# Three small tiles laid behind eight operand tiles, and a norm factor kept in PSUM, in an attention and feed-forward kernel on Trainium2

## The chip, the cores and the metric

The kernel runs on one core of a Trainium2 chip, in one launch. The metric is the device time of the launch in microseconds (us), lower is better. The engines have short names: PE (TensorE) multiplies, PEld is its loading of weights, DVE (VectorE) and ACT (ScalarE) work on tiles, POOL (GpSimd) too, and SP (SyncE) issues the DMAs.

## The reference

Three parts follow each other. First is attention in which a query sees only the keys of its own cluster; its output is laid out as 1536 tokens by 512. The two feed-forward parts are, cut to what matters:

```python
def _moe_ref(x, w_in, w_out):                    # w_in 512 x 2048, w_out 2048 x 512
    h = x @ w_in
    g = np.where(h >= 1, h, np.where(h <= -1, 0.0, (h + 1) ** 2 / 4))
    return g @ w_out

def _moe2_ref(x, w_gate, w_val, w_out, rms_g):   # w_gate, w_val 512 x 1536, w_out 1536 x 512
    rms = np.sqrt(np.mean(x * x, axis=-1, keepdims=True) + 1e-06)
    xn = x / rms * rms_g
    g = xn @ w_gate
    silu = g * (1.0 / (1.0 + np.exp(-g)))
    return (silu * (xn @ w_val)) @ w_out
```

## The kernel before

All inputs are float32. A matmul of the feed-forward parts is made of three in a reduced float format: each operand is split into a high and a low part, and high x high, high x low and low x high are added in PSUM. So `proj` (L577) makes one 128 x 512 block of `h` from 12 matmuls: four slices of the 512 features, three products each. The 1536 tokens stand in three blocks of 512; XH and XL hold the high and low part of the activations.

A split weight slice, or a split block of activations between the two matmuls of a part, lies in an operand place: 128 partitions x 2 x 512 words, which is 4096 bytes of a partition. There are 26. Eighteen are cut out of the tiles `aa` and `bb` that attention used; the other eight, `place0` to `place7`, are tiles of their own in the pool `pf`. That pool is opened when attention ends, on the memory that attention's tiles had (`reuse_waits="tile"`: who first writes a new tile waits for the last users of the old tiles under it). Before the places the pool holds the running output `Y` (24576 bytes of a partition), and three small tiles: `gain` (16 bytes, the four columns of rms_g), `eps6` and `ones` (4 bytes each). Each takes a slot of 32 bytes. Behind the places come the tiles `a`, `raw`, `mid`, `bits` and `s`.

A weight slice arrives by two DMAs from SP's queue (`raw` and `mid`, L509 and L511) and is split by five DVE instructions and one of ACT (L524 to L540). A scheduler written by hand interleaves these with the units of matmuls; the order of every engine is fixed when the program is built, and the engines are held together by semaphores.

Between the two feed-forward parts stands the norm. For each block of 512 tokens, ACT squares the four slices of Y (L700), POOL adds them into one tile `s` (L706), ACT and POOL split the sum (L708, L709), and `norm_unit` lets PE add over the partitions with a matmul by ones into a PSUM bank `ssq` (L716). From it ACT makes a first value of the factor 1/rms in `s` (L722, L723, between two loads of its function table, L746), and DVE refines it by one Newton step (L728 to L730). `scale_unit` multiplies the four slices of Y by the gain and the factor (DVE, L737), and ACT and POOL split them into XH and XL (L738, L739). Block 0's scaling stands among the last units of the first part, blocks 1 and 2 among the first units of the second. A unit of the second part computes a gate and a value block (two PSUM banks of the four with tag `h`) and closes with ACT's sigmoid (L595), two multiplications of DVE (L599 with the gate's bank, L600 with the value's), and the split (L602 on ACT, L606 on DVE). The bank `ssq` is one of the four with tag `y`.

Of the kernel before, what the change touches and what calls it, by code (L numbers as in the profile page):

```python
# [10 lines left out]
F32R = mybir.dt.float32r  # L11
BF16 = mybir.dt.bfloat16
AF = mybir.ActivationFunctionType
ALU = mybir.AluOpType
# [15 lines left out]
NPLACES = 26  # L30
# [7 lines left out]
def clustered_attention_two_ffn(  # L38
# [14 lines left out]
    nc = tc.nc  # L53
# [65 lines left out]
    st = {}  # L119
# [342 lines left out]
    a, b, c = prep(0), prep(1), prep(2)  # L462
# [26 lines left out]
    free = []  # L489
# [204 lines left out]
    def block(x, j, b):  # L694
        return x[:, j, BLK * b:BLK * b + BLK]
# [15 lines left out]
    def norm_unit(b):  # L711

        total = fp["tp"](f"ssq{b}")
        pace["rate"] = 0.9
        for n, x in enumerate((XH, XL)):
            nc.tensor.matmul(total, fp["ones"].to_broadcast([128, 128]), block(x, 0, b), start=(n == 0), stop=(n == 1))  # L716
        r = st["r", b] = st["sq", 4 * b]

        def first():
            if b == NB - 1:  # L720
                tables("natural_log_exp_and_others")
            nc.scalar.activation(r, total, AF.Ln, bias=fp["eps6"], scale=1.0 / DM)  # L722
            nc.scalar.activation(r, r, AF.Exp, scale=-0.5)  # L723
            if b > 0:
                tables("sigmoid_and_others")

        def newton():
            nc.vector.scalar_tensor_tensor(total, total, DM * 1e-6, r, op0=ALU.add, op1=ALU.mult)  # L728
            nc.vector.scalar_tensor_tensor(total, total, 0.5 / DM, r, op0=ALU.mult, op1=ALU.mult)
            nc.vector.scalar_tensor_tensor(r, total, 1.5, r, op0=ALU.subtract, op1=ALU.mult)  # L730

        later.insert(0, (first, newton))

# [11 lines left out]
    def tables(name):  # L745
        nc.scalar.preload_act_table_set(name)  # L746

    def units():
# [14 lines left out]
        def norm(b):  # L763
            return (lambda: norm_unit(b), 0.45, 2.04, [], 0)
# [327 lines left out]
    pf = ctx.enter_context(tc.tile_pool(name="ffn", bufs=1, reuse_waits="tile"))  # L1092
    psf = ctx.enter_context(tc.tile_pool(name="psf", bufs=1, space=PSUM, reuse_waits="tile"))
    fp["Y"] = pf.tile([128, 4 * NB, 512], F32, name="Y")
    fp["gain"] = pf.tile([128, 4], F32, name="gain")
    nc.sync.dma_start(fp["gain"], rms_g)
    nc.scalar.mul(fp["gain"], fp["gain"], -1.0)
# [1 line left out]
    nc.gpsimd.memset(fp["eps6"], 1e-6)  # L1099
    fp["ones"] = pf.tile([128, 1], F32R, name="ones")  # L1100
    nc.scalar.copy(fp["ones"], ones[:, 0:1])
    for j in range(NPLACES - 18):
        t = pf.tile([128, 2, 512], F32R, name=f"place{j}")
        free.append(t)
    fp["raw"] = lambda n: (pf.tile([128, 512, 2], U32, tag="raw", bufs=2, name=f"raw{n}"),
                           pf.tile([128, 512, 2], U32, tag="mid", bufs=2, name=f"mid{n}"),
                           pf.tile([128, 512], U32, tag="bits", bufs=2, name=f"bits{n}"))
# [53 lines left out]
```

## Time and profile before

| | |
|---|---|
| median of 3 runs | 805.37 us (804.75 to 807.14) |
| the profiled execution | 807.06 us |
| its span | 805.3 us |
| PE busy | 793.1 us, 98% of the span |
| DVE busy | 576.9 us, 72% |
| ACT busy | 361.0 us, 45% |
| POOL busy | 201.2 us, 25% |

The span is what the profile covers; 1.8 us of the execution lie outside it. A line such as L577 is a line of the kernel; in the changed kernel the lines from L718 on stand one or more lines later. [...]

### The profile page before, as it was taken

Reading aid. Unit: us, or ns where it says so; the run is one execution under the profiler, and the core shown is the slowest. Engines: PE = TensorE matmul, PEld = TensorE weight load, DVE = VectorE, ACT = ScalarE, POOL = GpSimd, SP = SyncE. Lnnn points to the kernel's source line nnn. Section 1 sums busy time; section 2 is a strip of 40 time slices with the busy share of each in tenths; the row PEclk is TensorE's granted clock in tenths of the full one; section 3 lists DMA queues with packets and bytes.
Section 4 is the critical chain, followed back from the end, with each engine's and each line's share of the span. In section 5 each row is a group of like instructions: output and inputs, shape, how many; then the busy total and the mean of one; then the engine's idle time right before and its main releaser. Section 6 shows DMA issues by size and latency. Waiting matters only on the chain.

```text
span 805.3 us, 10599 instructions
## 1 busy us (share of the span) xinstructions
PE 793.1 (98%) x3744; PEld 603.1 (75%) x3744; DVE 576.9 (72%) x1045; ACT 361.0 (45%) x667; POOL 201.2 (25%) x211
## 2 busy tenths in 40 slices
PE   9999999999999999999999999899999999999998
PEld 4665676676568888888888887678888888888887
DVE  6766787776676878777788689798877778733333
ACT  6675767665566654334443545533333222211110
POOL 4877999997000000000000233420000000000000
PEclk9999999999999999999999999999999999999999
DMA  7667665581342655444344423125655444100003
GB/s 196 164 143 169 153 166 125 138 221 34 105 131 78 189 173 163 157 155 152 111 157 130 132 78 136 48 92 174 205 187 178 157 157 155 54 1 1 0 28 129
DMA packets 32676, 103.13 MB, mean 128 GB/s; under 512 B 5144, under 2 KB 5484, under 8 KB 32624
## 3 DMA queue, kind: packets, MB, share of 16 engines
q1 hardware_dynamic: 32624, 102.46, 42.6%
q8 instruction: 29, 0.48, 0.2%
q14 instruction: 23, 0.19, 0.1%
HBM read 80.76 MB, written 3.15 MB: 104 GB/s over the span
## 4 chain that ended last, share of the span: by engine, by line
PE 82%; DVE 10%; ACT 5%; DMA 1%; issue 1%; POOLq 0%; POOL 0%; SPq 0%; DVEq 0%; ACTq 0%
PE h L577 32%; PE pv L397 7%; PE mp L333 4%; PE sc L376 4%; PE y L651 4%; PE y L650 4%; PE y L625 4%; PE y L652 4%; PE y L624 4%; PE y L623 4%; PE sc L377 4%; DVE Y L737 1%; PE sum L416 1%; DVE a L597 1%; DMA kraw<-kT 1%
## 5 line engine op out<-in xcount | busy, mean ns | idle before, releaser
L577 PE MATMUL h<-xh,aa 128*128 128x512 f32 x408 | 131.3, 394 | 2.6 <-DVE a L599 2.5
L335 DVE TENSOR_REDUCE M<-mp 128x1 f32<-128x384 f32 x186 | 94.5, 551 | 46.5 <-PE mp L333 46.2
L389 POOL TENSOR_TENSOR acc<-acc,P 128x384 f32<-128x384 f32 x112 | 109.2, 1006 | 4.3 <-ACT P L379 3.5
L379 ACT ACTIVATE P<-sc 128x384 f32<-128x384 f32 x192 | 82.6, 490 | 43.4 <-PE sc L377 36.1
L577 PE MATMUL h<-xh,place 128*128 128x512 f32 x288 | 94.3, 397 | 0.7 <-DVE a L599 0.7
L577 PEld LDWEIGHTS h<-xh,aa 128*128 128x128 f32 x408 | 77.2, 189 | 21.6 <-DVE a L599 3.3
L528 ACT ACTIVATE raw<-raw 128x512 f32<-128x512 f32 x62 | 42.2, 681 | 103.9 <-DVE bits L526 98.8
L577 PE MATMUL h<-xh,bb 128*128 128x512 f32 x264 | 85.1, 390 | 0.3 <-DVE bb L540 0.3
L577 PE MATMUL h<-xl,aa 128*128 128x512 f32 x204 | 80.2, 393 | 0.7 <-POOL xl L739 0.7
L706 POOL TENSOR_TENSOR s<-s,sq 128x512 f32<-128x512 f32 x9 | 12.0, 1334 | 270.7 <-ACT sq L700 270.0
L397 PE MATMUL pv<-P,v 128*64 128x384 f32 x384 | 70.6, 492 | 0.0
L597 DVE SCALAR_TENSOR_TENSOR a<-h,a 128x512 f32<-128x512 f32 x48 | 33.2, 691 | 47.8 <-ACT a L593 47.7
L376 PE MATMUL sc<-aa,bb 112*128 112x384 f32 x192 | 66.6, 347 | 0.0
L377 PE MATMUL sc<-aa,bb 97*128 97x384 f32 x192 | 65.1, 339 | 0.8 <-DMA aa<-mt 0.8
L577 PEld LDWEIGHTS h<-xh,place 128*128 128x128 f32 x288 | 54.2, 188 | 14.0 <-DVE a L599 1.0
L577 PEld LDWEIGHTS h<-xh,bb 128*128 128x128 f32 x264 | 49.5, 188 | 11.1 <-DVE bb L540 0.7
L577 PE MATMUL h<-xl,place 128*128 128x512 f32 x144 | 57.0, 396 | 0.0
L333 PE MATMUL mp<-bb,aa 112*128 112x384 f32 x186 | 52.4, 359 | 0.1
L577 PE MATMUL h<-xl,bb 128*128 128x512 f32 x132 | 51.4, 389 | 0.0
L397 PEld LDWEIGHTS pv<-P,v 128*64 128x64 f32 x384 | 25.4, 136 | 31.5 <-issue 30.6
L526 DVE SCALAR_TENSOR_TENSOR bits<-raw,bits 128x512 uint32<-128x512 uint32 x68 | 47.3, 696 | 1.5
L667 DVE TENSOR_TENSOR Y<-y,Y 128x512 f32<-128x512 f32 (+1 forms) x37 | 25.1, 677 | 31.5 <-PE y L652 31.4
(283 smaller groups left out, 1626.0 us busy)
## 6 DMA issues: line engine op xcount, KB each, us to landing
raw<-w_out SPq DMA_DIRECT2D x28, 512.0 KB
mid<-w_out SPq DMA_DIRECT2D x28, 511.8 KB
raw<-w_in SPq DMA_DIRECT2D x16, 512.0 KB
mid<-w_in SPq DMA_DIRECT2D x16, 511.8 KB
raw<-w_gate SPq DMA_DIRECT2D x12, 512.0 KB
raw<-w_val SPq DMA_DIRECT2D x12, 512.0 KB
mid<-w_gate SPq DMA_DIRECT2D x12, 511.8 KB
mid<-w_val SPq DMA_DIRECT2D x12, 511.8 KB
```

The costliest lines, as they stand in the source:

```text
L333: nc.tensor.matmul(mp, A[0:112, h, 0, 128 * qt:128 * qt + 128], Bk[0:112, h, 0, HALF * n:HALF * n + HALF], start=True, stop=True)
L335: nc.vector.tensor_reduce(st["M2", p][:, j, n:n + 1], mp, axis=AX.X, op=ALU.max)
L376: nc.tensor.matmul(sc, Bk[0:112, h, 0, ks], A[0:112, h, 0, qs], start=True, stop=False)
L377: nc.tensor.matmul(sc, Bk[0:97, h, 1, ks], A[0:97, h, 1, qs], start=False, stop=True)
L379: nc.scalar.activation(P, sc, AF.Exp, scale=0.125)
L389: nc.gpsimd.tensor_tensor(acc, acc, P, op=ALU.add)
L397: nc.tensor.matmul(pv[64 * h:64 * h + 64, 0:HALF], st["v", p][:, h, kt], st["P", p, i, h], start=(kt == 0), stop=(kt == NT - 1))
L526: nc.vector.scalar_tensor_tensor(t, hi, 0xC0000000, t, op0=ALU.bitwise_and, op1=ALU.bitwise_or)
L528: nc.scalar.activation(hi.bitcast(F32), hi.bitcast(F32), AF.Square, scale=2.0 ** 15)
L577: nc.tensor.matmul(h, w[:, wi, fs], x[:, kc, cs], start=(n == 0), stop=(n == 11))
L597: nc.vector.scalar_tensor_tensor(a, hs[0], 1.0, a, op0=ALU.max, op1=ALU.min)
L623: nc.tensor.matmul(y, w[:, 0, js], g[:, 0], start=(m == m0), stop=False)
```

## The change

Two edits. The three small tiles are laid out behind the eight places. And for the blocks 1 and 2 the last of the three Newton instructions writes its result to the PSUM bank `ssq` in which it already works, where `scale_unit` then reads it; for block 0 it still goes to `s` in SBUF.

```diff
@@ norm_unit
-        r = st["r", b] = st["sq", 4 * b]
+        r = st["sq", 4 * b]
+        R = st["r", b] = total if b else r
...
         def newton():
             nc.vector.scalar_tensor_tensor(total, total, DM * 1e-6, r, op0=ALU.add, op1=ALU.mult)
             nc.vector.scalar_tensor_tensor(total, total, 0.5 / DM, r, op0=ALU.mult, op1=ALU.mult)
-            nc.vector.scalar_tensor_tensor(r, total, 1.5, r, op0=ALU.subtract, op1=ALU.mult)
+            nc.vector.scalar_tensor_tensor(R, total, 1.5, r, op0=ALU.subtract, op1=ALU.mult)
@@ the pool of the feed-forward part
     fp["Y"] = pf.tile([128, 4 * NB, 512], F32, name="Y")
+    for j in range(NPLACES - 18):
+        t = pf.tile([128, 2, 512], F32R, name=f"place{j}")
+        free.append(t)
     fp["gain"] = pf.tile([128, 4], F32, name="gain")
     nc.sync.dma_start(fp["gain"], rms_g)
...
     fp["ones"] = pf.tile([128, 1], F32R, name="ones")
     nc.scalar.copy(fp["ones"], ones[:, 0:1])
-    for j in range(NPLACES - 18):
-        t = pf.tile([128, 2, 512], F32R, name=f"place{j}")
-        free.append(t)
```

In the built programs the addresses within a partition are these. `place0` begins at byte 165504 before and at 165408 after, and the other seven follow at steps of 4096. `gain` goes from 165408 to 198176, `eps6` and `ones` with it. Everything else stays: XH at 17952, XL at 42528, `aa0` at 67104, the other five of `aa` and `bb` at steps of 12288, `raw`, `mid`, `bits`, `a` and `s` where they were. XH, XL, all `aa` and `bb` and their slices, and `place0` to `place7` after the change, start at 1568 beyond a multiple of 4096; the places before started at 1664, which is 96 bytes farther.

No instruction moves on any engine. The waits differ at a few. On SP, where attention ends and the pool's first DMAs are issued (`raw_3178` is the raw tile of weight slice 6, the first in the new pool):

```order
 L509 DMA raw_2984<-w_out 128x1024 [waits DMAHW5_49,DMAHW1_49,DVE_49]
 L511 DMA mid_2985<-w_out 128x2047 [waits DMAHW6_49,DMAHW2_49,DVE_49]
-L1096 DMA gain<-rms_g 128x4
-L509 DMA raw_3178<-w_in 128x1024 [waits PE_49]
+L1100 DMA gain<-rms_g 128x4 [waits PE_49,Pool_49]
+L509 DMA raw_3178<-w_in 128x1024 [waits Pool_49]
 L511 DMA mid_3179<-w_in 128x2047 [waits DMAHW5_49,DVE_49,Activation_49]
 L509 DMA raw_3184<-w_in 128x1024
```

The DMA of `gain` now waits for a matmul, and the raw DMA behind it no longer does. By the value that the semaphore must reach, the matmul is the first of the two that add up the tile of exponentials P of attention's last head pair for its key tile 10 of 12 (L405). The memset of `eps6` on POOL has the same new wait, and one for ACT; no wait of PE, ACT or DVE changes, in its engine or in its value.

On DVE, at the norm of block 1 (`ssq_5078` is its PSUM bank, `s_4886` its SBUF tile):

```order
 L536 SCALAR_TENSOR_TENSOR bb_106<-raw_5005,bits_5007 128x512 [waits Activation_49]
 L538 TENSOR_SCALAR bits_5007<-bb_106 128x512 [waits DVE_49]
-L728 SCALAR_TENSOR_TENSOR ssq_5078<-ssq_5078,s_4886 128x512 [waits Activation_49]
-L729 SCALAR_TENSOR_TENSOR ssq_5078<-ssq_5078,s_4886 128x512 [waits DVE_49]
-L730 SCALAR_TENSOR_TENSOR s_4886<-ssq_5078,s_4886 128x512 [waits DVE_49]
-L737 SCALAR_TENSOR_TENSOR Y<-Y,gain,s_4886 128x512 [waits DVE_49]
-L737 SCALAR_TENSOR_TENSOR Y<-Y,gain,s_4886 128x512 x2
+L729 SCALAR_TENSOR_TENSOR ssq_5078<-ssq_5078,s_4886 128x512 [waits Activation_49]
+L730 SCALAR_TENSOR_TENSOR ssq_5078<-ssq_5078,s_4886 128x512 [waits DVE_49]
+L731 SCALAR_TENSOR_TENSOR ssq_5078<-ssq_5078,s_4886 128x512 [waits DVE_49]
+L738 SCALAR_TENSOR_TENSOR Y<-Y,gain,ssq_5078 128x512 [waits DVE_49]
+L738 SCALAR_TENSOR_TENSOR Y<-Y,gain,ssq_5078 128x512 x2
```

The five instructions stand where they stood; the last Newton instruction writes the bank and the scaling reads it. The scaling had two large inputs in SBUF (Y and s), and has one in SBUF and one in PSUM.

## Rows read from the trace of the kernel before

**Rows 1.** Busy us by stage: window, length, then each engine's us (instructions).
```profile
262.06:451.50 189.44, 189.44 (x826) 155.02 (x827) 147.61 (x268) 87.40 (x140) 1.53 (x2) 1.00 0.49 155
451.50:539.43 87.93, 82.59 (x343) 64.65 (x342) 73.76 (x104) 43.52 (x69) 32.12 (x23) 0.98 0.26 86
539.43:777.10 237.67, 237.67 (x1035) 194.10 (x1034) 157.54 (x273) 59.12 (x98) 0.00 (x0) 1.00 0.34 110
```

**Rows 2.** Chain that ended last, runs of h matmuls: start us, length us, what.
```profile
360.74 8.16 PE h L577 x36
377.28 8.42 PE h L577 x36
636.39 16.87 PE h L577 x72
661.62 16.32 PE h L577 x72
```

**Rows 3.** The page's costliest groups: h matmuls with a place as weights.
```profile
L577 PE MATMUL h<-xh,place 128*128 128x512 f32 x288 | 94.3, 397 | 0.7 <-DVE a L599 0.7
L577 PE MATMUL h<-xl,place 128*128 128x512 f32 x144 | 57.0, 396 | 0.0
```

**Rows 4.** Three DVE lines: durations in ns (least/median/most), first and last start.
```profile
L526 DVE SCALAR_TENSOR_TENSOR bits<-raw,bits x68: 678/692/1179, 201.0 to 694.6; 128x512 uint32<-128x512 uint32 x68
L728 DVE SCALAR_TENSOR_TENSOR ssq<-ssq,s x3: 690/692/693, 462.0 to 518.3; 128x512 f32<-128x512 f32 x3
L737 DVE SCALAR_TENSOR_TENSOR Y<-Y,gain,s x12: 735/1016/1798, 466.6 to 533.3; 128x512 f32<-128x512 f32 x12
```

**Rows 5.** DVE in order of time: start us, length us, what.
```profile
475.53 0.68 DVE L633 TENSOR_TENSOR Y<-y,Y 128x512 f32<-128x512 f32 x1
476.13 1.18 DVE L526 SCALAR_TENSOR_TENSOR bits<-raw,bits 128x512 uint32<-128x512 uint32 x1
...
504.62 3.65 DVE L737 SCALAR_TENSOR_TENSOR Y<-Y,gain,s 128x512 f32<-128x512 f32 x3
```

**Rows 6.** POOL in order of time.
```profile
473.64 3.12 POOL L739 TENSOR_TENSOR xl<-Y,xh 128x512 fp32r<-128x512 f32 x2 [1.28 <-ACT xh L738]
...
504.06 1.29 POOL L706 TENSOR_TENSOR s<-s,sq 128x512 f32<-128x512 f32 x1 [2.89 <-ACT sq L700]
506.08 1.63 POOL L709 TENSOR_TENSOR xl<-s,xh 128x512 fp32r<-128x512 f32 x1 [0.73 <-ACT xh L708]
...
531.31 3.26 POOL L739 TENSOR_TENSOR xl<-Y,xh 128x512 fp32r<-128x512 f32 x2 [5.58 <-ACT xh L738]
```

**Rows 7.** Chain that ended last, from the norm of block 1 on: start us, length us, what.
```profile
508.19 0.69 DVE a L599
...
516.54 0.70 DVE a L599
...
533.42 1.71 DVE Y L737
...
539.09 5.97 PE h L577 x25
```

**Rows 8.** PE in order of time, three first matmuls of a unit.
```profile
508.92 0.50 PE L577 MATMUL h<-xh,place 128*128 128x512 f32 x1 [0.66 <-DVE a L599]
...
517.29 0.50 PE L577 MATMUL h<-xh,aa 128*128 128x512 f32 x1 [2.50 <-DVE a L599]
...
535.78 0.50 PE L577 MATMUL h<-xh,aa 128*128 128x512 f32 x1
```

**Rows 9.** ACT's first sigmoid of the second part, in order of time.
```profile
505.91 0.59 ACT L595 ACTIVATE a<-h 128x512 f32<-128x512 f32 x1
```

**Rows 10.** PE's last sums of exponentials, and SP's queue there, in order of time.
```profile
233.06 0.81 PE L405 MATMUL sum<-P,ones 128*64 128x384 f32 x4
...
234.26 0.42 SPq L1096 DMA_DIRECT2D gain<-rms_g  x1
...
247.67 0.33 SPq L511 DMA_DIRECT2D mid<-w_in  x1
```

## The prediction

> **What bounds the kernel now.** I read the chain that ended last first. From 262 us to 451.5 us it is PE alone, from there to 539 us it runs over DVE, ACT and POOL (the norm and what stands around it), and from 539 us to the end it is PE again. The busy times by stage say the same: PE is busy in all of the first and third stage, while DVE has a fifth and a third of them free, and in the middle one PE idles 5.3 us of 87.9 [rows 1]. So in the outer stages only a faster or shorter PE counts, and in the middle one only what shortens the DVE, ACT and POOL chain. Each edit bears on one of the two kinds of stage.
>
> Next I read the chain's runs of h matmuls against each other. The 36 that begin at 360.74 us have weights in `aa` and take 8.16 us, 226.7 ns each; the 36 at 377.28 us have `place0` and take 8.42 us, 233.9 ns. The 72 at 661.62 us, all `aa`, take 16.32 us, 226.7 ns; the 72 at 636.39 us, all on places, take 16.87 us, 234.3 ns [rows 2]. The same work on the same engine at a granted clock of 1.00 [rows 1] is 7.2 to 7.6 ns slower per matmul when the weights lie in a place. It is so in every unit of the trace, hundreds of us apart and with different traffic beside it, so it belongs to the place.
>
> What is special about the places is in the addresses: XH, XL, `aa` and `bb` all start 1568 bytes beyond a multiple of 4096, and their slices lie at multiples of 512 from there; the places start 96 bytes farther. So in a matmul with `aa` the moving operand and the weights differ by a multiple of 512, and in one with a place by that and 96.
>
> **Term 1, the places.** The change puts all eight at 1568 beyond a multiple of 4096, like the others. I take it that the distance between the two operands' addresses makes the 7 ns, and that all matmuls then run at 226.7 ns. The h matmuls on places are 288 + 144 = 432 [rows 3], at 7.3 ns 3.2 us. Units of y have places among weights, activations or both, so I count by stage instead. First stage: 826 matmuls at 226.7 ns are 187.2 us, and it lasts 189.44 [rows 1]: 2.2 us too much. Third: 1035 matmuls are 234.6 us, and it lasts 237.67: 3.1 us. A window also counts the matmul cut by its edge; with one or two fewer in each, the surplus is up to 0.4 us larger each. I take 2.4 and 3.3, with 5.3 and 6.2 us as the bounds of the sum. The last 28 us to the end give some 0.2 more. In the middle stage a faster PE only waits longer, so I take nothing. DVE must follow the faster PE: it has 42 us free of 189 and 80 of 238.
>
> A gain of nothing is the other bound: no run with shifted places is in the trace.
>
> **Term 2, the factor in PSUM.** Eight scalings (L737 for blocks 1 and 2) change one input. An undisturbed one takes 735 ns, but the longest takes 1798 [rows 4]. The long ones are those beside a POOL operation: three from 504.62 us take 3.65 us [rows 5], while POOL works from 504.06 to 505.35 and from 506.08 to 507.71 us [rows 6]. That it is the second SBUF input that waits is seen elsewhere: while POOL works from 473.64 to 476.76 us [rows 6], the addition at 475.53 us, one input in PSUM and one in SBUF, takes 0.68 us, and the one at 476.13 with both in SBUF takes 1.18 [rows 5]. With the factor in PSUM the scaling is of the first kind, and I take 735 ns for each.
>
> A price the other way is a PSUM input by itself. L526 reads two SBUF tiles in 692 ns, L728 a PSUM bank and an SBUF tile in 692 [rows 4]: nothing. [...]
>
> What it moves, link by link:
>
> *Block 1.* Three scalings take 3 x 0.735 = 2.2 us instead of 3.65, so L599 behind them starts 1.5 us earlier, near 506.7 instead of 508.19 us [rows 7]. Its other input, ACT's sigmoid, ends at 506.50 us [rows 9], so it is not late. L599 frees an `h` bank: PE's wait before 508.92 us, 0.66 by the view [rows 8], goes. Then ACT's chain (split of the unit, three casts of the scaled Y, table load, Ln, Exp, table load, sigmoid) stands between L600 and the L599 at 516.54 us [rows 7], each waiting for the one before, and shifts by the same 1.5 us. PE's start at 517.29 us, which waits 2.50 us for that L599 [rows 8], comes at 515.8. It still waits, since the unit before ends earlier too.
>
> *Block 2.* The scaling at 533.42 us takes 1.71 us beside POOL's two operations from 531.31 to 534.57 us [rows 6, 7]. With 0.7 it frees 1.0 us. Behind it are L599, L600, ACT's split and cast, and POOL's last part of XL, for which PE waits at 539.09 us [rows 7]. That part then ends 1.5 + 1.0 = 2.5 us earlier, near 536.6. PE would ask for it at about 536.4 (its unit starts at 535.78 us [rows 8] less 1.5 to 1.7, and ten matmuls of 226.7 ns come first), so it goes on within 0.2 us of that. The two-SBUF-input L606 just ahead keeps its stall, as do block 0's scalings. Bounds: 0 if the stall stays, 2.9 if the collisions that are left fall better.
>
> **What costs nothing.** The bank `ssq` is held until the last scaling, but the next y units stand behind all nine units of the second part's first slices, and no wait of PE changes. On SP the DMA of `gain` now waits for a sum on PE, with the raw and mid DMAs of slice 6 and all later weights queued behind it. PE's very last sums start at 233.06 us and take 0.81, and `gain` was issued at 234.26 us without the wait [rows 10]: the wait is over before it is reached. The mid DMA is held until 247.67 us by DVE in any case [rows 10], which covers 13 us should it come late. The memset on POOL has only the norm's sums behind it, over 200 us later.
>
> **Sum.** 2.4 + 2.5 + 3.3 + 0.2 = 8.4 us, against the profiled execution of 807.06 us: 798.7. That execution was 1.7 us above the median of its runs, 805.37; the same 8.4 us from the median gives 797.0 us, 1.0% less. I forecast 797.0, with 795.7 to 798.5 as this case's own range.
>
> **Rivals.**
> *A, the scalings stay as slow* (the gain's column is still an SBUF input beside Y, and no row shows a PSUM input with such a column beside a working POOL; or the freed DVE meets POOL elsewhere). Only term 1: 805.4 - 5.9 = 799.5 us.
> *B, the placement is without effect*, and the 7 ns come with something else that stays with the places. PE's two reads would then not disturb each other. [...] Rows 2 speak against it, since nothing but the tile differs. Only term 2: 802.9 us.
> *C, neither*: the change does not do what it says, 805.4 us.
> *D, slower*: what counts is not the distance of the operands but where the places start. They leave multiples of 128 bytes (165504) for 32 beyond one (165408). If the 7 ns is the price of an operand off such a line beside one that is on it in the wrong order, it could double when both are off: 5.9 us more in the PE stages, 2.5 less in the middle: 808.8 us. It decides from 2.5 us of added PE time on. Against it: with `aa` and XH both are 32 beyond such a line, and that is the fast pair.
>
> **How the numbers follow.** The forecast's case has 0.70: rows 2 show the effect large and steady, the chain of the norm is followed step by step, but neither is tried in the trace. A has 0.13, B 0.08, C 0.05, D 0.04. The range 795.2 to 801.0 us holds the forecast's case nearly whole and A, 0.8 in all; B, C and D lie above. A change under 0.3% (2.4 us) can't be told from none in this kernel. Faster by more: 0.70 + 0.13 and half of B, whose 802.9 lies on the bound, 0.87; within: half of B and C, 0.09; slower: D, 0.04.
>
> **What would show it.** Term 1: runs of 72 h matmuls on places at 16.3 us like the others, and the first stage shorter by 2.4 us. Term 2: no scaling of blocks 1 and 2 above 0.8 us, L599 right behind the third, and 2.5 us between the end of the first stage and PE's restart after POOL's last part. A is right if scalings of 1.7 us remain; B if the place runs keep 8.4 and 16.9 us; D if the `aa` runs or the place runs grow. The forecast is wrong too if PE, faster in the outer stages, begins to wait there for DVE.

## The result, and the profile after

The changed kernel takes 797.74 us (median of 3 runs, 797.36 to 798.60) against 805.37, a ratio of 0.9903 with 0.9875 to 0.993 as the 95% interval (the ratios here go by all runs kept, not by the two medians). Timed again later beside other kernels it took 796.44 us against 805.01, 0.9892 (0.9875 to 0.991). Forecast were 797.0 us, 8.4 us less; measured are 7.6 and 8.6 less. One execution among the experiments, the first of the kernel with the second edit alone, took 2003 us with PE busy for 1997 of them; its profile has no row of PE's granted clock and why it was slow is not known, so it is left out, and that kernel was profiled again.

The profiled execution after takes 797.36 us, its span is 795.6. I begin with the chain that ended last. Its runs of h matmuls answer to [rows 2]; the columns are start us, length us, what.

```profile
375.06 8.16 PE h L577 x36
...
629.11 16.32 PE h L577 x72
```

These are the two runs on places. They took 8.42 and 16.87 us and now take 8.16 and 16.32, the length that those on `aa` had and have. On the page the h matmuls with a place as weights answer to [rows 3]: 397 and 396 ns have become 389. These lengths overlap, 389 ns where the run of 72 above gives 226.7 ns a matmul, so the pace is read from the runs.

```profile
L577 PE MATMUL h<-xh,place 128*128 128x512 f32 x288 | 92.1, 389 | 0.0
...
L577 PE MATMUL h<-xl,place 128*128 128x512 f32 x144 | 56.0, 389 | 0.0
```

For the scalings, now L738, the view of that line (durations in ns: least, median, most; first and last start) answers to [rows 4]. The eight with the factor in PSUM all take 735 to 748 ns; block 0's four, which kept it in SBUF, still reach 1781.

```profile
L738 DVE SCALAR_TENSOR_TENSOR Y<-Y,gain,ssq x8: 735/743/748, 501.3 to 528.4; 128x512 f32<-128x512 f32 x8
L738 DVE SCALAR_TENSOR_TENSOR Y<-Y,gain,s x4: 739/1260/1781, 463.3 to 470.1; 128x512 f32<-128x512 f32 x4
```

That this is not because POOL fell silent is seen in POOL's instructions in order of time, which answer to [rows 6]. The three scalings from 501.30 us overlap with its work from 500.73 and from 502.75 us.

```profile
500.73 1.29 POOL L706 TENSOR_TENSOR s<-s,sq 128x512 f32<-128x512 f32 x1 [2.88 <-ACT sq L700]
502.75 1.30 POOL L709 TENSOR_TENSOR xl<-s,xh 128x512 fp32r<-128x512 f32 x1 [0.73 <-DVE Y L738]
...
526.40 3.27 POOL L740 TENSOR_TENSOR xl<-Y,xh 128x512 fp32r<-128x512 f32 x2 [5.58 <-ACT xh L739]
```

DVE in the same order answers to [rows 5]: three scalings in 2.06 us where they took 3.65, and one at 528.44 us that lies wholly beside POOL's work and takes 0.74. Between them stands the view's best control: L606, which reads two SBUF tiles, takes 1.79 us beside the same POOL instruction.

```profile
501.30 2.06 DVE L738 SCALAR_TENSOR_TENSOR Y<-Y,gain,ssq 128x512 f32<-128x512 f32 x3
503.28 0.69 DVE L599 TENSOR_TENSOR a<-h,a 128x512 f32<-128x512 f32 x1
...
526.73 1.79 DVE L606 TENSOR_TENSOR bb<-a,bb 128x512 fp32r<-128x512 f32 x1
528.44 0.74 DVE L738 SCALAR_TENSOR_TENSOR Y<-Y,gain,ssq 128x512 f32<-128x512 f32 x1
```

In the chain of waits the links of [rows 7] then stand earlier: L599 at 503.28 (508.19 before) and 511.64 us (516.54), and PE's restart behind POOL's last part of XL at 533.16 (539.09).

```profile
448.54 0.70 DVE Y L633
...
503.28 0.70 DVE a L599
...
511.64 0.70 DVE a L599
...
533.16 14.35 PE h L577 x62
```

Shifts in such a view add up what happened since the start, so they have to be taken apart. Three landmarks bound the stages: PE's last sums of exponentials, in attention and ahead of everything the change touches; the last addition to Y that the first stage ends with; and PE's restart. For the kernel before the first is in [rows 10] (233.06 us) and the third in [rows 7]; the second is this row of its chain:

```profile
451.91 0.70 DVE Y L633
```

After the change the last sums stand at 231.97 us, in PE's instructions in order of time:

```profile
231.97 0.81 PE L405 MATMUL sum<-P,ones 128*64 128x384 f32 x4
```

| us | before | after | difference | forecast |
|---|---|---|---|---|
| start to the last sums | 233.06 | 231.97 | -1.09 | 0 |
| to the end of the first stage | 218.85 | 216.57 | -2.28 | -2.4 |
| to PE's restart | 87.18 | 84.62 | -2.56 | -2.5 |
| to the end of the span | 266.2 | 262.4 | -3.8 | -3.5 |
| span | 805.3 | 795.6 | -9.7 | -8.4 |

The first line has nothing to do with the change: the same kernel profiled once more reaches the last sums at 231.08 us, 0.9 us earlier again, and the kernel with the second edit alone, whose tiles lie as before, at 232.07. Without it the difference is 8.6 us.

### The profile page after: what moved, and what is told of

It reads as the page before. It is cut to its first block, busy times and chain, and to the rows that moved or that the text cites. A ratio compares the mean times of both kernels' runs of the same rounds, so it can differ in the third digit from the quotient of the medians.

```text
span 795.6 us, 10601 instructions
## 1 busy us (share of the span) xinstructions
PE 783.5 (98%) x3744; PEld 602.6 (76%) x3744; DVE 573.5 (72%) x1045; ACT 360.6 (45%) x667; POOL 200.7 (25%) x211
## 4 chain that ended last, share of the span: by engine, by line
PE 82%; DVE 9%; ACT 5%; DMA 2%; issue 1%; POOL 1%; POOLq 0%; SPq 0%; DVEq 0%; ACTq 0%
PE h L577 32%; PE pv L397 7%; PE mp L333 5%; PE sc L376 4%; PE y L650 4%; PE y L625 4%; PE y L652 4%; PE y L623 4%; PE y L651 4%; PE y L624 4%; PE sc L377 4%; PE sum L416 1%; DVE a L597 1%; DMA kraw<-kT 1%; DVE Y L738 1%
## 5 line engine op out<-in xcount | busy, mean ns | idle before, releaser
L577 PE MATMUL h<-xh,place 128*128 128x512 f32 x288 | 92.1, 389 | 0.0
L706 POOL TENSOR_TENSOR s<-s,sq 128x512 f32<-128x512 f32 x9 | 12.1, 1341 | 234.2 <-ACT sq L700 233.6
L526 DVE SCALAR_TENSOR_TENSOR bits<-raw,bits 128x512 uint32<-128x512 uint32 x68 | 47.4, 696 | 1.5
```

What stands on the lines that cost most here:

```text
L526: nc.vector.scalar_tensor_tensor(t, hi, 0xC0000000, t, op0=ALU.bitwise_and, op1=ALU.bitwise_or)
L577: nc.tensor.matmul(h, w[:, wi, fs], x[:, kc, cs], start=(n == 0), stop=(n == 11))
```

## The experiments

All are variants of the changed kernel or of the one before, each compared with the kernel before on the same chip. None leaves computation out.

### Each edit alone

The first edit alone:

```diff
-        R = st["r", b] = total if b else r
+        R = st["r", b] = r
```

> The changed kernel with the factor of all three blocks left in SBUF, so that only the order of the tiles differs from the kernel before. My theory (two independent terms): the h runs on places of 72 matmuls take 16.3 us like the others and the time falls by term 1 alone, 2.4 + 3.3 + 0.2 = 5.9 us, to about 799.5 us where before has 805.4; scalings of blocks 1 and 2 up to 1.8 us remain. Rival B (placement without effect, the time came from elsewhere): 16.9 us runs, 805.4 us. A second rival (the gain of the places is partly swallowed because the norm's chain, not PE, sets the middle): less than 4 us gained.

Measured: 799.31 us against 805.11, ratio 0.9922 (0.9908 to 0.9935), 5.8 us less. Its chain:

```profile
375.07 8.16 PE h L577 x36
...
448.55 0.70 DVE Y L633
...
535.77 14.35 PE h L577 x62
```

The runs on places are fast, and from the end of the first stage to PE's restart it takes 87.22 us, as before (87.18). Rival B fell: the order of the tiles alone gives term 1, all of it.

The second edit alone is the kernel before with the factor in PSUM for blocks 1 and 2:

```diff
-        r = st["r", b] = st["sq", 4 * b]
+        r = st["sq", 4 * b]
+        R = st["r", b] = total if b else r
...
-            nc.vector.scalar_tensor_tensor(r, total, 1.5, r, op0=ALU.subtract, op1=ALU.mult)
+            nc.vector.scalar_tensor_tensor(R, total, 1.5, r, op0=ALU.subtract, op1=ALU.mult)
```

> The kernel before with the factor of blocks 1 and 2 in PSUM, and nothing else. My theory: about 2.5 us less than before, 802.9 us; the eight scalings of blocks 1 and 2 at 735 to 750 ns, the first L599 behind them 1.5 us earlier against the end of the first stage, PE's restart 2.5 us earlier, and the place runs still 8.4 and 16.9 us. Rival (the terms are not independent, or the freed time is lost in a later wait): within 1 us of before although the scalings are short.

Measured: 802.64 us (median of the four runs kept; 802.98 with the fifth) against 805.11, ratio 0.9962 (0.9949 to 0.9976) by the four. Once more, for a profile:

> The kernel before with the factor of blocks 1 and 2 in PSUM once more, for its profile: its first profiled execution took 2003 us. Theory: about 2.1 to 2.5 us less than before; scalings of blocks 1 and 2 at 735 to 750 ns, L599 behind the three scalings 1.5 us earlier against the end of the first stage, PE's restart 2.5 us earlier, h runs on places still 8.4 us (36) and 16.9 us (72). Rival (with the slower places PE is later in the middle, so that part of the 2.5 us is hidden): PE's restart 1.0 to 1.5 us earlier.

Measured: 801.75 us against 805.01, ratio 0.9967 (0.9955 to 0.9978), 3.3 us less. From the new profile's chain:

```profile
376.31 8.42 PE h L577 x36
...
450.94 0.70 DVE Y L633
...
505.61 0.69 DVE a L599
...
535.48 14.52 PE h L577 x62
...
632.77 16.87 PE h L577 x72
```

Its eight scalings take 733 to 749 ns. The runs on places keep 8.42 and 16.87 us. From the end of the first stage it is 54.67 us to the L599 behind the scalings (56.28 before, 1.61 less) and 84.54 to PE's restart (87.18, 2.64 less). The rival fell: nothing of the middle's gain hangs on PE being faster. The two edits are independent: alone 2.64 in the middle, with the first edit 2.56, and the first edit alone moves the middle by 0.04.

### What about the places is slow

Six layouts tell a distance from an address. In the first, everything starts where the slow places of the kernel before stood:

```diff
+    cp.tile([128, 24], F32, name="pad96")
     XH = cp.tile([128, 4, TOK], F32R, name="xh")
     XL = cp.tile([128, 4, TOK], F32R, name="xl")
```

> The changed kernel with a tile of 96 bytes that nothing uses laid ahead of XH, so that XH, XL, aa, bb and the places all start 96 bytes farther, at 1664 beyond a multiple of 4096, the place where the slow tiles of the kernel before stood. Theory (only the distance between the two operands of a matmul counts): nothing changes, all runs of h at 226.7 ns a matmul, within 1 us of the changed kernel's 797.7. Rival (the start on that address itself is slow): all feed-forward matmuls at 234 ns, some 15 us more, 812 us.

Measured: 796.66 us against 804.98, ratio 0.9895 (0.9873 to 0.9917). Its chain (lines stand one later here):

```profile
374.46 8.16 PE h L578 x36
...
628.51 16.32 PE h L578 x72
```

All runs are fast at the very address that was slow for the places alone. Rival D, a price of the start itself, fell.

In the second, XH and XL are the ones that stand apart from `aa` and `bb`. These move down by 49152 bytes, 12 times 4096, and so still start 1568 beyond a multiple of 4096:

```diff
-    XH = cp.tile([128, 4, TOK], F32R, name="xh")
-    XL = cp.tile([128, 4, TOK], F32R, name="xl")
...
+    cp.tile([128, 24], F32, name="pad96")
+    XH = cp.tile([128, 4, TOK], F32R, name="xh")
+    XL = cp.tile([128, 4, TOK], F32R, name="xl")
```

> The changed kernel with XH and XL laid out behind the tiles aa and bb, and a tile of 96 bytes that nothing uses between, so that XH and XL start 96 bytes farther than before against a multiple of 512, and aa, bb and the places do not. Theory (the distance of the two operands modulo 512 makes the 7 ns): every h matmul, with aa, bb or a place, now has operands 96 bytes apart and runs at about 234 ns; some 1440 h matmuls times 7.3 ns less those hidden in the middle, about 8 to 10 us more than the changed kernel. If only one sign of the distance counts (the weights 96 bytes beyond the moving operand, as in the kernel before, but not the reverse): no change. Rival (a property of the places' own addresses): no change either in the aa runs, 226.7 ns.

Measured: 805.96 us against 805.11, ratio 1.0012 (1.0001 to 1.0024), so 8.2 to 9.5 us more than the changed kernel in its two timings. The built program shows one thing that the expectation had wrong: the extra 96 bytes move the places too, so that they stand 96 bytes from `aa` and `bb`, but at no distance from XH and XL. The chain shows this, and it makes the test sharper:

```profile
360.64 8.41 PE h L578 x36
377.44 8.19 PE h L578 x36
...
635.02 16.37 PE h L578 x72
659.75 16.80 PE h L578 x72
```

The middle two runs are those on places, the others those on `aa`. It is the picture of [rows 2] turned round: `aa`, at the same 1568 beyond a multiple of 4096, goes from 8.16 and 16.32 to 8.41 and 16.80 us (233.6 and 233.3 ns a matmul), the places, at their old slow address, to 8.19 and 16.37 (227.5 and 227.4). In these runs of h neither tile is slow; the pair is, with the weights starting 96 bytes short of the moving operand (modulo 512) as with them 96 bytes beyond it.

The next three, and a fourth after their result, put a tile of 32, 128, 64 and 256 bytes ahead of the places, as in:

```diff
     fp["Y"] = pf.tile([128, 4 * NB, 512], F32, name="Y")
+    pf.tile([128, 8], F32, name="pad32")
     for j in range(NPLACES - 18):
```

> The changed kernel with a tile of 32 bytes ahead of the places, so that places and XH, XL, aa, bb are 32 bytes apart (modulo 512) where they were 96 before the change and 0 after. If any distance but a multiple of 512 is slow: place runs of h near 234 ns. If the distance counts modulo 64: slow too, since 96 and 32 are the same then. If the price grows with the distance: about a third of the 7.3 ns, 229 ns.

> The same with 128 bytes. If any distance but a multiple of 512 is slow: place runs of h near 234 ns. If the distance counts modulo 64 or modulo 128: 226.7 ns. If the price grows with the distance: about 236 ns.

> The same with 64 bytes. If any distance but a multiple of 512 is slow, or if it counts modulo 128: place runs of h near 234 ns. If it counts modulo 64: 226.7 ns. If the price grows with the distance: about 231.5 ns.

> The changed kernel with a tile of 256 bytes ahead of the places. With 32, 64, 96 and 128 bytes the place runs of h were slow (232.6 to 234 ns). If any distance but a multiple of 512 is slow: 232 to 234 ns again, about 802 us. If the distance counts modulo 256: 226.7 ns, about 797.7 us.

Measured in single executions: 803.20, 801.98, 803.03 and 796.60 us, in this order. The longer run on places in the four chains, 32 bytes first:

```profile
632.69 16.80 PE h L577 x72
```

128 bytes:

```profile
631.68 16.72 PE h L577 x72
```

64 bytes:

```profile
632.32 16.80 PE h L577 x72
```

256 bytes:

```profile
628.38 16.32 PE h L577 x72
```

Per matmul that is 233.3, 232.2, 233.3 and 226.7 ns. The price does not grow with the distance, and it doesn't count modulo 64 or 128, by which two or one of the slow ones would have been fast. It is gone at 256, so my "any distance but a multiple of 512 is slow" fell too: what was tried fits a distance modulo 256.

The units of y show that the pair is not the whole rule. In some of their matmuls both operands are places, which lie at multiples of 512 from each other, and yet these were slow before the change and are fast after it. One such group by line, before and then after (the last figure but one is the mean length in ns):

```profile
L625 PE MATMUL y<-place,place 128*128 128x512 f32 x28 | 11.1, 395 | 0.0
L625 PE MATMUL y<-place,place 128*128 128x512 f32 x28 | 10.9, 389 | 0.0
```

PE in order of time in one such unit of the kernel before:

```profile
313.74 0.40 PE L623 MATMUL y<-place,place 128*128 128x512 f32 x1
...
315.13 0.39 PE L623 MATMUL y<-aa,bb 128*128 128x512 f32 x1
...
316.52 0.40 PE L623 MATMUL y<-place,place 128*128 128x512 f32 x1
```

From 313.74 to 316.52 us stand twelve matmuls, six with two places and then six with two operands out of `aa` and `bb`. None has operands that differ by 96 bytes modulo 512, and still the twelve take 2.78 us, 232 ns each; after the change they take 2.72 us, 227 each. What sets them apart from a run on `aa` alone is that matmuls on places and matmuls on `aa` and `bb` follow each other. So the price is not confined to the matmul whose own operands stand apart; how far it reaches, and from which operand, no run shows. After the change, with all starts equal modulo 256, there is no such difference left: the chain's runs of 36 and of 72 h matmuls take 8.16 and 16.32 us, 226.7 ns a matmul, whatever tile they read.

### Block 0 as well

The factor of block 0 had stayed in SBUF, and two of its scalings stand in the changed kernel's chain with 1.70 us. Here all three blocks use PSUM; block 0's bank then has to come from the `h` banks.

```diff
-        R = st["r", b] = total if b else r
+        R = st["r", b] = total
...
-    fp["tp"] = lambda name: psf.tile([128, 512], F32, tag="y", bufs=4, name=name)
+    fp["tp"] = lambda name: psf.tile([128, 512], F32, tag="h" if name == "ssq0" else "y", bufs=4, name=name)
```

> The changed kernel with the factor in PSUM for block 0 too; block 0's bank is taken from the tag of the h banks, since a y unit that needs its bank comes before the scaling ends. Theory (a large SBUF input beside a working POOL is what stalls): block 0's four scalings go from up to 1.8 us to 735 to 750 ns, and the two of 1.7 us that stand in the chain of the changed kernel at 464.98 and 467.87 us give back about 1 us each at most: 1.2 us less than the changed kernel (0.6 to 2.1). Rival: the h bank that is held, or PE's own queue, takes their place in the chain: no gain or up to 1 us lost, with short scalings all the same.

Measured: 793.27 us against 805.11, ratio 0.9859 (0.9839 to 0.9879), 4.5 us under the changed kernel's first median. The chain there, first of the changed kernel:

```profile
464.98 1.70 DVE Y L738
...
467.87 1.70 DVE Y L738
...
471.43 0.84 DVE bits L524
```

and of this one:

```profile
449.23 0.70 DVE Y L633
...
465.66 0.66 DVE Y L738
...
467.51 0.66 DVE Y L738
...
470.03 0.46 DVE bits L524
...
531.38 14.37 PE h L577 x62
```

The two stalls give 2 x 1.04 us and L524 behind them 0.38, 2.46 together; the middle takes 82.15 us instead of 84.62, 2.47 less. So all of it reaches PE, and my 1.2, which gave half away to later waits for no reason that a row showed, was too little; the rival fell as well. But 4.5 us are more than the trace holds, so both kernels were timed side by side:

> The changed kernel as it is, to stand beside the next one on the same chip in the same rounds: 797.7 us, within 0.8.

> The changed kernel with the factor of all three blocks in PSUM, once more beside the changed kernel itself. By the two traces the middle is 2.5 us shorter (two scalings of 1.70 us became 0.66, and one split of 0.84 us 0.46): 795.2 us, 2.5 us under the run beside it. The rival to that reading is the first median, 793.27 us, 4.5 us under the changed kernel's 797.74: more than the middle's stalls hold, so a gain outside the middle would have to be found, or else two of the microseconds were the start of the kernel, which varies from run to run.

Measured: 796.44 and 794.08 us, against 805.01 (0.9892, 0.9875 to 0.991; and 0.9864, 0.9849 to 0.9879). The difference is 2.4 us, that of the trace; the new profile's middle, from 447.40 to 529.56 us in its chain, is 82.16. The other 2 us of the first comparison did not come back, so I take them for the scatter of runs made at different times. At 793 to 794 us this is the fastest version here, faster than both kernels of the case.

## Why the prediction was right

**Term 1, the places.** Forecast 2.4 + 3.3 + 0.2 us, measured 2.28 in the first stage and 3.8 from PE's restart to the end. With the first edit alone the two stretches are 216.58 us (231.97 to 448.55; the sums stand at 231.97 there too) and 262.4 (798.2 less 535.77), the same as with both. The step from [rows 2], that the 7 ns belong to the distance between the operands and not to the place, was argued in the prediction and is now shown for runs of h in both directions: `aa` becomes slow at its old offset, and the places become fast at their old address. Its wording was too narrow, since 256 does as well as 512, and it left out that matmuls of y with two places, whose distance is right, were slow too. The sum did not hang on that, because it counted what whole stages took beyond 226.7 ns a matmul. The bounds, 5.3 and 6.2 with 0.2 for the end, hold the 6.1 measured.

Rival B took the placement to be without effect. The runs show otherwise: 226.7 against 232 to 234 ns a matmul in runs of h that differ in the distance of the two operands alone. Why the pace hangs on it is not shown by any run and stays open.

**Term 2, the factor in PSUM.** Forecast 1.5 + 1.0 us. From the end of the first stage to the L599 behind the scalings it is 54.74 us instead of 56.28, 1.54 less; to PE's restart 1.02 more are gained. PE's wait of 0.66 us for the first of these L599 [rows 8] is gone, and the next is 2.10 us instead of 2.50. Rival A had its doubt in the gain's column, a second SBUF input of 4 bytes a partition. Eight scalings at 735 to 748 ns, those from 501.30 and at 528.44 us beside a working POOL, and twelve at 733 to 748 in the kernel with all three blocks, settle it: the column doesn't count, only a second large input does. L606 with two SBUF tiles keeps its stall, 1.79 us (1.78 before), as forecast.

**PSUM as an input by itself.** The prediction took it to be free, from the equal 692 ns of L526 and L728. The shortest scaling from PSUM takes 735 ns and the shortest from SBUF took 735 [rows 4], so no price shows here either.

**What costs nothing.** SP issues the DMA of `gain` right behind the mid DMA ahead of it, the next raw right behind that, and the mid DMA of slice 6 at 246.59 us, 1.08 earlier than in [rows 10], as much as the last sums:

```profile
232.79 0.33 SPq L511 DMA_DIRECT2D mid<-w_out  x1
233.21 0.38 SPq L1100 DMA_DIRECT2D gain<-rms_g  x1
233.65 0.42 SPq L509 DMA_DIRECT2D raw<-w_in  x1
246.59 0.33 SPq L511 DMA_DIRECT2D mid<-w_in  x1
```

PE, faster in the outer stages, doesn't wait for DVE there: the windows of the changed kernel for the first and the last stage (length, then PE, PEld, DVE, ACT and POOL busy, granted clock, DMA share, GB/s) show it busy in all of both, and in the last its 234.84 us are 226.7 ns for each of 1036 matmuls.

```profile
262.00:448.54 186.54, 186.54 (x824) 154.54 (x823) 146.47 (x266) 87.30 (x140) 1.89 (x2) 1.00 0.49 157
...
533.16:768.00 234.84, 234.84 (x1036) 194.51 (x1037) 157.94 (x274) 58.94 (x98) 0.00 (x0) 1.00 0.35 112
```

**The sum.** 8.4 forecast, 8.6 in the trace without the 1.09 us of attention, 7.6 and 8.6 by the two pairs of medians. The one term that was a little small is the last stretch, 3.5 where it measured 3.8. What the prediction did not reckon with is the scatter of attention between executions, about 1 us, as large as a term.

## What to carry to other kernels

Where the same matmul has two paces, compare the addresses of its two operands before looking for traffic: here 96 bytes of small tiles ahead of the places set the pace of the runs that read them, 233.9 and 234.3 ns a matmul against 226.7. The cure was to let all operand tiles start equal modulo 256, and with the first edit alone no stage grew by more than 0.04 us. For a vector instruction beside a working GpSimd, one large SBUF input with the other in PSUM is worth trying wherever a factor already passes through a bank: here scalings of up to 1798 ns became 735 to 748, with the column of scalars left in SBUF. And count a stall on a chain that nothing else shortens whole, unless a row names the wait that takes its place: in block 0 the 2.46 us of stalls were worth 2.47 us of the middle.

## What was not expected of the hardware

The price of the distance is a step: in runs of h, 32, 64, 96 and 128 bytes cost 5.5 to 7.6 ns a matmul of 226.7, and 0 and 256 none. Between 128 and 256 only the 96 bytes short were tried, which are 160 if it counts modulo 256; they cost 6.6 to 6.9 ns.

In the changed kernel's first profile PE's granted clock fell after it had stood idle for 2.10 us ahead of its start at 512.39 us. That start, and the window behind it:

```profile
512.39 0.76 PE L577 MATMUL h<-xh,aa 128*128 128x512 f32 x1 [2.10 <-DVE a L599]
```

```profile
513.00:515.00 2.00, 2.00 (x6) 1.60 (x5) 1.93 (x5) 1.63 (x3) 0.62 (x1) 0.50 0.00 0
```

At 0.50 the six matmuls of this window keep PE busy for all of its 2.00 us. The profile of the kernel before has the same fall, 0.50 from 519 to 521 us, behind its wait of 2.50 us. The changed kernel's second profile shows 1.00 from 505 to 521 us, after a wait of 2.12 us ahead of the same matmul at 511.50; one window of it, in which six matmuls keep PE busy for 1.25 us:

```profile
513.00:515.00 2.00, 1.25 (x6) 0.74 (x5) 1.93 (x4) 0.92 (x2) 1.27 (x1) 1.00 0.00 0
```

It made no difference: from the end of the first stage to PE's restart the one takes 84.62 us and the other 84.61 (447.65 to 532.26 in its chain), because PE waits for the last part of XL in both.
